# Linear attention before a balanced expert layer: k and v with six rows of every head in 96 partitions

## The chip, the cores and the metric

The kernel runs on one core of a Trainium2 chip. Times are device microseconds of that core; a kernel's time is the median of its runs, and the kernel before has 727.41 us (727.30 to 731.44 in three runs). A core has a matrix engine (TensorE, PE in the profile, with its weight loads as PEld), VectorE (DVE), ScalarE (ACT), GpSimd (POOL) and SyncE (SP), which in this kernel issues the plain transfers. Every engine works through its own list of instructions in order and waits at semaphores for the others. Sixteen DMA engines move the data between HBM and the on-chip SBUF; matmuls write to PSUM.

## The reference

```python
# q, k, v: (8, 8, 576, 64): batch, heads, sequence, head_dim
kv  = np.einsum('bhsd,bhse->bhde', k, v)          # 64 x 64 for each of the 64 heads
out = np.einsum('bhsd,bhde->bhse', q, kv)
rms = np.sqrt(np.mean(out * out, axis=-1, keepdims=True) + 1e-06)
x   = (out / rms * g_norm).transpose(0, 2, 1, 3).reshape(4608, 512)
logits = x @ w_gate                                # 8 experts
# the (token, expert) pairs in falling order of logit; an expert takes 576 tokens at most
assigned = greedy_balanced(logits)
out[assigned == e] = np.maximum(x[assigned == e] @ w1[e], 0) @ w2[e]   # 512 -> 1024 -> 512
```

All is float32.

## The kernel before

It has two stages. The attention stage (up to about 130 us) makes the normalised rows and their gate logits and writes both to `x_dram`; the expert stage finds thresholds for the balanced assignment, gathers each expert's tokens and runs the two layers. The change lies in the attention stage.

`load` brings k, v and q of one batch in two halves each (half of the heads), 576 KB a transfer, in the order k, v, q, k, v, q, all from SyncE. `paced` lets a transfer start only when the one three places before it has landed. A tile has 128 partitions: a pair of heads r, 64 partitions for each head of the pair, and nine sequence rows in every partition. Each of the three names has two buffers, so the loads of batch b+2 are issued at the end of `prepare(b)`, and wait until the matmuls and transposes of batch b have read the buffers.

`prepare(b)` makes what the tiles of batch b need. For each pair of heads it adds up kv in PSUM (L306): the left operand is a 64x64 block of k, the right one of v, and head l of the pair works in its own half of the rows of the matrix engine; even and odd sequence rows j go to the two halves of the columns, so a matmul uses a quarter of the array and the sums of the odd rows end in the upper partitions. ACT copies those down (`odd`, L312), DVE adds (`kv`, L314), and two GpSimd copies (L320) put the sum into both partition halves of `kvx`, the operand of the output matmuls. Four transposes of kv (`t_ps`, L325), an ACT copy (`kvt`, L327) and eight small matmuls with the gate weights (`w_ps`, L333) give kv times gate, which a DVE copy (L335) puts beside kv in `kvx`. `turn_q` transposes q in five pieces (`qt_ps`, L294) that ACT or DVE copies to `qt`. All pieces of PSUM called "tr" share two buffers.

`tiles` makes the output: for each tile of 128 tokens 16 matmuls of 64x64 blocks (`o_ps`, L363), ACT's square and copy (`sq` L369, `o_sb` L370), DVE's sum (`ms` L371), and, once a batch, the norm, the logits and a GpSimd copy of the inverse norm (L388). Head block `9r+j` of `qt` lies in the lower or upper 64 partitions by its parity, which is why kv must stand in both halves.

On PE, DVE, ACT and SP the order is the one in which the program is written: between the tiles of batch b, `prepare(b+1)` advances by one piece at each `yield`, and its rest is done after the last tile. Writes of `o_sb` to `x_dram` are put off: `writes` holds them until there are `2*LAG`, with `LAG + 1` buffers of `o_sb`. The gate weights are loaded on ACT's queue, scaled by g (L116), and a first matmul on PE (`g2_ps`, L198) uses them for a bound on the logits.

Of the kernel before, what the change touches and what calls it, by code (L numbers as in the profile page):

```python
# [7 lines left out]
FT = mybir.dt.float32  # L8
# [3 lines left out]
AL = mybir.AluOpType  # L12
# [3 lines left out]
P = 128  # L16
# [9 lines left out]
def kernel(  # L26
# [11 lines left out]
    nc = tc.nc  # L38
    PS = bass.MemoryType.PSUM

    B, H, S, D = q.shape
    N, DM = out.shape
    E, _, F = moe_w1.shape
    CAP = N // E
    NP = H // 2
    HP = P // 2
    R = S // HP
    GC = N // P
    DC = DM // P
    FC = F // P  # L50
    W = D + E
    NB = (CAP + P - 1) // P
    HALF = CAP // 2
    assert D == HP and R * HP == S and R == 9 and NP == 4 and B % 2 == 0 and GC * P == N and HALF <= 512

    const = ctx.enter_context(tc.tile_pool(name="const", bufs=1, side="left"))
    asg = ctx.enter_context(tc.tile_pool(name="asg", bufs=1, side="left"))
# [4 lines left out]
    att = att_cm.__enter__()  # L64
    psa_cm = tc.tile_pool(name="ps_att", bufs=1, space=PS)
    psa = psa_cm.__enter__()


    loaded = {}
# [3 lines left out]
    def paced(dma):  # L73

        if len(issued) >= AHEAD:
            tc.add_manual_dep(dma.ins, issued[-AHEAD].name,
                              mybir.DependencyInfo(mybir.DependencyClass.Sync, mybir.DependencyReason.DATA),
                              reason="paced loads")
        issued.append(dma.ins)

    def load(name, b, h):

        if h == 0:
            loaded[name, b] = att.tile([P, NP, R, D], FT, name=f"{name}_sb", tag=name, bufs=2)
        rs = slice(h * NP // 2, (h + 1) * NP // 2)
        src = {"k": k, "v": v, "q": q}[name]
        paced(nc.sync.dma_start(
            loaded[name, b][:, rs].rearrange("p r j d -> p r (j d)"),
            src[b].rearrange("h s d -> (h s) d").rearrange("(r p j) d -> p r (j d)", r=NP, j=R)[:, rs]))

    for b in range(2):
        for h in range(2):
# [3 lines left out]
    g_col = const.tile([P, 1], FT, name="g_col")  # L96
    for l in range(2):
        nc.scalar.dma_start(g_col[l * D:(l + 1) * D, :], g_norm.rearrange("(d o) -> d o", o=1))
    gw = const.tile([P, NP, 2, E], FT, name="gw")
    nc.vector.memset(gw, 0.0)  # L100
    for l in range(2):
        ls = slice(l * D, (l + 1) * D)
        nc.scalar.dma_start(gw[ls, :, l, :], moe_w_gate.rearrange("(r p) e -> p r e", p=P)[ls])


    iota_p_i = const.tile([P, 1], I32, name="iota_p_i")
# [7 lines left out]
    ident = const.tile([P, P], FT, name="ident")  # L114
    nc.vector.tensor_scalar(ident, in0=row_f, scalar1=iota_p, scalar2=None, op0=AL.is_equal)
    nc.vector.tensor_scalar(gw.rearrange("p r l e -> p (r l e)"), in0=gw.rearrange("p r l e -> p (r l e)"),  # L116
                            scalar1=g_col, scalar2=None, op0=AL.mult)
    eps = const.tile([P, 1], FT, name="eps")
    nc.vector.memset(eps, EPS)

# [55 lines left out]
    nine, rem, to_row, to_half = (col_at[:, n] for n in range(4))  # L176
    nc.vector.tensor_scalar(nine, in0=row_f[:, 0:GC + 1], scalar1=R - 0.5, scalar2=None, op0=AL.is_gt)
    for i in range(2, B // 2):
# [9 lines left out]
    nc.vector.tensor_tensor(rise, col_at[:, 2:4, 1:GC + 1], col_at[:, 2:4, 0:GC], op=AL.subtract)  # L188


    gsq = asg.tile([P, NP * 2 * E], FT, name="gsq")
    nc.vector.tensor_tensor(gsq, gw.rearrange("p r l e -> p (r l e)"), gw.rearrange("p r l e -> p (r l e)"), op=AL.mult)
    g2 = asg.tile([P, E], FT, name="g2")
    nc.vector.reduce_sum(out=g2, in_=gsq.rearrange("p (a e) -> p e a", e=E), axis=AXX)
    ones_f = asg.tile([P, P], FT, name="ones_f")
    nc.vector.memset(ones_f, 1.0)
    g2_ps = psa.tile([P, E], FT, name="g2_ps", tag="tr", bufs=2)
    nc.tensor.matmul(g2_ps, lhsT=ones_f, rhs=g2, start=True, stop=True)  # L198
    bound = asg.tile([P, 1], FT, name="bound")
    nc.vector.tensor_reduce(bound, g2_ps, axis=AXX, op=AL.max)  # L200
    nc.scalar.activation(bound, bound, ACT.Sqrt)
# [1 line left out]
                            op0=AL.mult, op1=AL.add)  # L203
# [10 lines left out]
    for s in range(NSTEP):  # L214
        nc.vector.tensor_scalar(away[:, s], in0=row_f[:, 0:NCAND + 1], scalar1=span,
                                scalar2=part_of[s], op0=AL.mult, op1=AL.mult)
# [62 lines left out]
    turned_q, kv_of = {}, {}  # L279

    def prepare(b):

        k_sb, v_sb = loaded.pop(("k", b)), loaded.pop(("v", b))

        q_sb = loaded.pop(("q", b)).rearrange("p r j d -> p (r j d)")
        NT = NP * R // 2
        qt = att.tile([P, NT, P], FT, name="qt", tag="qt", bufs=3)
        turned_q[b] = qt

        def turn_q(n):  # L290
            m = min(4, NT - 4 * n)
            t_ps = psa.tile([P, 4, P], FT, name="qt_ps", tag="tr", bufs=2)
            for x in range(m):
                nc.tensor.transpose(t_ps[:, x, :], q_sb[:, (4 * n + x) * P:(4 * n + x + 1) * P], ident)  # L294
            if n in (1, 2):
                nc.vector.tensor_copy(qt[:, 4 * n:4 * n + m], t_ps[:, 0:m])
            else:
                nc.scalar.copy(qt[:, 4 * n:4 * n + m], t_ps[:, 0:m])


        kv_ps = psa.tile([P, 2, 512], FT, name="kv_ps", tag="kv")
        for r in range(NP):
            for j in range(R):
                for l in range(2):
                    ls, cs = slice(l * D, (l + 1) * D), slice(j % 2 * D, (j % 2 + 1) * D)
                    nc.tensor.matmul(kv_ps[cs, l, r * D:(r + 1) * D], lhsT=k_sb[ls, r, j, :], rhs=v_sb[ls, r, j, :],  # L306
                                     start=(j < 2), stop=(j >= R - 2))
            if r < 2:
                turn_q(r)
                yield  # L310
        odd = att.tile([D, 2, NP * D], FT, name="odd", tag="odd")
        nc.scalar.copy(odd, kv_ps[D:P, :, 0:NP * D])  # L312
        kv = att.tile([D, NP, 2, D], FT, name="kv", tag="kv")
        nc.vector.tensor_tensor(kv.rearrange("p r l d -> p l r d"),  # L314
                                kv_ps[0:D, :, 0:NP * D].rearrange("p l (r d) -> p l r d", d=D),
                                odd.rearrange("p l (r d) -> p l r d", d=D), op=AL.add)

        kvx = att.tile([P, H, W], FT, name="kvx", tag="kvx", bufs=3)
        for n in range(2):
            nc.gpsimd.tensor_copy(kvx[n * D:(n + 1) * D, :, 0:D], kv.rearrange("p r l d -> p (r l) d"))  # L320
        yield
        turn_q(2)
        t_ps = psa.tile([P, NP, D], FT, name="t_ps", tag="tr", bufs=2)
        for r in range(NP):
            nc.tensor.transpose(t_ps[:, r, :], kv[:, r].rearrange("p l d -> p (l d)"), ident[0:D, 0:D])  # L325
        kvt = att.tile([P, NP, D], FT, name="kvt", tag="kvt")
        nc.scalar.copy(kvt, t_ps)  # L327
        yield
        turn_q(3)
        w_ps = psa.tile([P, NP, 2 * E], FT, name="w_ps", tag="tr", bufs=2)  # L330
        for r in range(NP):
            for n in range(2):
                nc.tensor.matmul(w_ps[n * D:(n + 1) * D, r], lhsT=kvt[:, r, :],  # L333
                                 rhs=gw[:, r].rearrange("p l e -> p (l e)"), start=True, stop=True)
        nc.vector.tensor_copy(kvx[:, :, D:W], w_ps.rearrange("p r (l e) -> p (r l) e", l=2))  # L335
        kv_of[b] = kvx
        turn_q(4)
        if b + 2 < B:
            for h in range(2):
                for name in "kvq":  # L340
                    load(name, b + 2, h)

    LAG = 5
    writes = []

    def tiles(c0, rows):
# [5 lines left out]
        for t, halves in enumerate(rows):  # L352


            o_ps = psa.tile([P, 2, 512], FT, name="o_ps", tag="o", bufs=2)
            for r2 in range(NP // 2):
                for l in range(2):
                    for rp in range(2):
                        for n, (bn, j) in enumerate(halves):
                            r = 2 * r2 + rp  # L360
                            block = R * r + j
                            ks = slice(block % 2 * D, (block % 2 + 1) * D)
                            nc.tensor.matmul(  # L363
                                o_ps[n * HP:(n + 1) * HP, rp, (2 * r2 + l) * W:(2 * r2 + l + 1) * W],
                                lhsT=turned_q[bn][ks, block // 2, l * HP:(l + 1) * HP],
                                rhs=kv_of[bn][ks, 2 * r + l], start=True, stop=True)
            o4 = o_ps[:, :, 0:NP * W].rearrange("p b (h w) -> p b h w", w=W)
            sq = att.tile([P, H, D], FT, name="sq", tag="sq")
            nc.scalar.activation(sq.rearrange("p (b h) d -> p b h d", b=2), o4[:, :, :, 0:D], ACT.Square, scale=D ** -0.5)  # L369
            nc.scalar.copy(o_sb[:, t].rearrange("p (b h) w -> p b (h w)", b=2), o_ps[:, :, 0:NP * W])  # L370
            nc.vector.reduce_sum(out=ms[:, t * H:(t + 1) * H], in_=sq, axis=AXX)  # L371
            yield
# [40 lines left out]
    with tc.manual_schedule(engines={PE, DVE, ACTE, SPE}):  # L413
        for _ in prepare(0):
            pass
        for b in range(B):
            parts = prepare(b + 1) if b + 1 < B else iter(())
            n = 0
# [368 lines left out]
```

## Time and profile before

| | us |
|---|---|
| median of the runs | 727.41 |
| the profiled execution | 728.39 |
| its span on the core | 726.6 |
| PE busy (share of the span) | 632.7 (87%) |
| DVE busy | 395.3 (54%) |
| ACT busy | 164.4 (23%) |
| POOL busy | 95.8 (13%) |

The profile is of one execution. Its page shows the busy share of each engine in 40 equal slices, the clock that TensorE was granted, and how busy the DMA engines were. The groups of instructions are named by line, engine, operation, output and operands, with the count, the busy time, the mean of one, and the idle time before them with what ended it ("issue" is idle time that no semaphore explains). A matmul of float32 appears as two records here, a transpose as one. In the attention stage (0 to 140 us) the groups are:

| line | what | count | mean ns |
|---|---|---|---|
| L306 | PE `kv_ps`, 64x64 | 1152 | 235 |
| L363 | PE `o_ps`, 64x72 | 1152 | 247 |
| L294 | PE `qt_ps`, 128x128 | 144 | 327 |
| L333 | PE `w_ps`, 128x16 | 128 | 234 |
| L325 | PE `t_ps`, 64x64 | 32 | 257 |
| L312 | ACT `odd`, 64x512 | 8 | 583 |
| L327 | ACT `kvt`, 128x256 | 8 | 375 |
| L314 | DVE `kv`, 64x512 | 8 | 683 |
| L296 | DVE `qt`, 128x512 | 16 | 678 |
| L335 | DVE `kvx`, 128x64 | 8 | 220 |
| L320 | POOL `kvx`, 64x512 | 16 | 608 |
| L388 | POOL `o_sb`, 128x32 | 9 | 240 |

A matmul's duration is that of one from start to end; several run at a time, so the starts of a run of them tell their pace: 36 `kv_ps` records from 22.22 to the next kind of work at 22.90, 32 `o_ps` records from 21.67 to 22.22, four `qt_ps` from 22.90 to 23.49.

### The profile page before, as it was taken

The numbers are of one execution on the slowest core, as the hardware profiler recorded it, in microseconds if no ns is written. First come the engines' busy times: TensorE is split into PE (matmuls) and PEld (weight loads), VectorE is DVE, ScalarE is ACT, GpSimd is POOL, SyncE is SP. The second block draws the span as 40 slices with busy tenths as digits, with TensorE's granted clock in tenths as the row PEclk, the third lists the DMA queues.
The fourth block names the chain that finished last, engine by engine and source line by source line (L and its number), as shares of the span: only waits on it lengthen the run. The fifth ranks groups of instructions, "written<-read, shape, count | busy, mean of one in ns | idle before, by whom it ended". The sixth has DMA issues, their size and how long they took to land.

```text
span 726.6 us, 12295 instructions
## 1 busy us (share of the span) xinstructions
PE 632.7 (87%) x4959; PEld 404.6 (56%) x4959; DVE 395.3 (54%) x1381; ACT 164.4 (23%) x331; POOL 95.8 (13%) x113
## 2 busy tenths in 40 slices
PE   3768686113999999999999999999999999999994
PEld 3656575002774576457546744774576467547641
DVE  4454656886677488748765874787478530010000
ACT  1555565001120211122112112210311122122100
POOL 0100100003002300410041013003100421010011
PEclk9998888555899999999999999999999999999998
DMA  8998888208106300910170045007200945010001
GB/s 290 307 298 287 285 306 312 81 0 259 46 1 229 136 5 1 331 39 1 57 292 23 1 166 197 9 0 275 96 1 3 345 148 179 15 43 8 0 30 36
DMA packets 41400, 93.34 MB, mean 128 GB/s; under 512 B 3456, under 2 KB 3456, under 8 KB 41344
## 3 DMA queue, kind: packets, MB, share of 16 engines
q1 hardware_dynamic: 34752, 72.49, 28.6%
q0 software_dynamic: 5888, 20.06, 7.9%
q8 instruction: 39, 0.64, 0.4%
q14 instruction: 17, 0.14, 0.1%
q10 hardware_dynamic: 704, 0.02, 0.1%
HBM read 72.50 MB, written 20.05 MB: 127 GB/s over the span
## 4 chain that ended last, share of the span: by engine, by line
PE 62%; issue 19%; DVE 11%; POOL 2%; ACT 2%; DMA 2%; ACTq 0%; POOLq 0%; DVEq 0%
PE y_ps L713 23%; PE h_ps L704 23%; PE y_ps L723 3%; PE qt_ps L294 3%; PE o_ps L363 3%; PE kv_ps L306 3%; DVE over L259 2%; PE t_ps L678 2%; PE n_ps L452 2%; POOL out_dram L685 1%; POOL xg L614 1%; DMA gw<-in_moe_w_gate_dram 1%; DVE need L458 1%; DVE ms L371 1%; DVE ends L490 1%
## 5 line engine op out<-in xcount | busy, mean ns | idle before, releaser
L704 PE MATMUL h_ps<-xt,w_sb 128*128 128x288 f32 x1024 | 264.1, 414 | 0.0
L713 PE MATMUL y_ps<-w_sb,hid 128*128 128x512 f32 x512 | 227.6, 595 | 0.0
L704 PEld LDWEIGHTS h_ps<-xt,w_sb 128*128 128x128 f32 x1024 | 191.9, 192 | 54.9 <-issue 5.7
L713 PEld LDWEIGHTS y_ps<-w_sb,hid 128*128 128x128 f32 x512 | 94.2, 190 | 100.8 <-issue 100.0
L707 ACT ACTIVATE hid<-h_ps 128x288 f32<-128x288 f32 x128 | 52.6, 411 | 216.7 <-PE h_ps L704 216.7
L685 POOL DMA_INDIRECT out_dram<-y_sb,outs x40 | 42.9, 1073 | 427.7 <-ACT y_sb L718 399.4
L667 DVE TENSOR_TENSOR xs<-xg 128x512 f32<-128x512 f32 (+1 forms) x40 | 27.4, 689 | 77.7 <-PE t_ps L678 60.0
L259 DVE TENSOR_TENSOR over<-mx,cand 128x1152 bf16<-128x1152 f32 (+3 forms) x52 | 67.0, 1289 | 1.6
L730 DVE TENSOR_TENSOR y_sb<-y_ps,y_part 64x512 f32<-64x512 f32 x8 | 5.5, 682 | 105.2 <-ACT y_part L729 105.2
L718 ACT COPY y_sb<-y_ps 128x512 f32<-128x512 f32 x32 | 18.7, 584 | 161.8 <-PE y_ps L713 161.8
L614 POOL DMA_INDIRECT xg<-x_dram,ids x40 | 39.8, 996 | 77.2 <-DVE at_row L628 35.9
L679 ACT ACTIVATE xt<-t_ps,g_col 128x512 f32<-128x512 f32 (+1 forms) x40 | 25.7, 645 | 95.1 <-PE t_ps L678 87.4
L363 PE MATMUL o_ps<-kvx,qt 64*64 64x72 f32 x1152 | 30.9, 247 | 10.8 <-issue 9.9
L452 PEld LDWEIGHTS <-over 128*128 128x128 bf16 x441 | 17.6, 97 | 40.8 <-DVE over L259 31.7
L452 PE MATMUL n_ps<-best,over 128*128 128x32 bf16 x441 | 19.3, 179 | 23.5 <-DVE over L259 21.0
L678 PEld LDWEIGHTS t_ps<-ident,xs 128*128 128x128 f32 (+1 forms) x160 | 19.6, 150 | 30.6 <-issue 23.1
L371 DVE TENSOR_REDUCE ms<-sq 128x8 f32<-128x512 f32 x36 | 24.0, 679 | 19.7 <-ACT sq L369 19.6
L363 PEld LDWEIGHTS o_ps<-kvx,qt 64*64 64x64 f32 x1152 | 25.0, 149 | 16.6 <-issue 14.8
L294 PE MATMUL qt_ps<-ident,q_sb 128*128 128x128 f32 x144 | 29.1, 327 | 5.3 <-ACT kvt L327 1.9
L306 PE MATMUL kv_ps<-v_sb,k_sb 64*64 64x64 f32 x1152 | 27.1, 235 | 7.5 <-issue 7.5
L490 DVE TENSOR_SCALAR ends<-from_lo,ends 32x2 f32<-32x2 f32 x144 | 31.6, 219 | 2.8
L678 PE MATMUL t_ps<-ident,xs 128*128 128x128 f32 (+1 forms) x160 | 25.0, 283 | 8.6 <-DVE xs L667 8.6
(171 smaller groups left out, 467.2 us busy)
## 6 DMA issues: line engine op xcount, KB each, us to landing
w_sb<-in_moe_w_dram SPq DMA_DIRECT2D x16, 1024.0 KB
w_sb<-in_moe_w_dram SPq DMA_DIRECT2D x8, 2048.0 KB
k_sb<-in_k_dram SPq DMA_DIRECT2D x16, 576.0 KB
v_sb<-in_v_dram SPq DMA_DIRECT2D x16, 576.0 KB
q_sb<-in_q_dram SPq DMA_DIRECT2D x16, 576.0 KB
x_dram<-o_sb SPq DMA_DIRECT2D x16, 576.0 KB
x_dram<-o_sb SPq DMA_DIRECT2D x4, 288.0 KB
xg<-x_dram,ids POOLq DMA_INDIRECT x40
```

The source lines that it names most:

```text
L259: nc.vector.tensor_tensor(over[:, c0:c1], mx[:, c0:c1].rearrange("p (c o) -> p c o", o=1).to_broadcast([P, c1 - c0, NCAND]), cand[:, 1:NCA ...
L294: nc.tensor.transpose(t_ps[:, x, :], q_sb[:, (4 * n + x) * P:(4 * n + x + 1) * P], ident)
L306: nc.tensor.matmul(kv_ps[cs, l, r * D:(r + 1) * D], lhsT=k_sb[ls, r, j, :], rhs=v_sb[ls, r, j, :], start=(j < 2), stop=(j >= R - 2))
L363: nc.tensor.matmul(o_ps[n * HP:(n + 1) * HP, rp, (2 * r2 + l) * W:(2 * r2 + l + 1) * W], lhsT=turned_q[bn][ks, block // 2, l * HP:(l + 1) ...
L452: nc.tensor.matmul(n_ps, lhsT=over[:, c:c + G].rearrange("p c n -> p (c n)"), rhs=best[:, :, c:c + G], start=(c == 0), stop=(c == GC - G))
L490: nc.vector.tensor_scalar(ends[g * QP:(g + 1) * QP], in0=from_lo, scalar1=lo_was[0:QP], scalar2=None, op0=AL.add)
L614: tokens = nc.gpsimd.indirect_dma_start(out=xg[0:nr].rearrange("p h w -> p (h w)"), out_offset=None, in_=x_dram, in_offset=bass.IndirectOf ...
L678: nc.tensor.transpose(t_ps[:, d, 0:nr], xs[0:nr, d * P:(d + 1) * P], ident[0:nr, 0:nr])
L685: put = nc.gpsimd.indirect_dma_start(out=out, out_offset=bass.IndirectOffsetOnAxis(ap=ids_of[t][0:nr, n:n + 1], axis=0), in_=y_sb[0:nr, :] ...
L704: nc.tensor.matmul(h_ps, lhsT=w1[:, 2 * (d % 2) + d // 2, f * P:(f + 1) * P], rhs=xt[:, d, cs], start=(d == 0), stop=(d == DC - 1))
L707: nc.scalar.activation(hid[:, f, cs], h_ps, ACT.Relu)
L713: nc.tensor.matmul(y_ps, lhsT=hid[:, f, a:a + nr], rhs=w2[:, f, :], start=(f == 0), stop=(f == FC - 1))
```

## The change

k and v are loaded with 96 partitions: six sequence rows of every head stand in one partition, for all eight heads. A kv matmul now sums over 96 rows at a time, six for a head instead of nine, and the two heads of a pair go to the two halves of the columns. So kv of head l of every pair ends in partition half l, and one DVE copy takes it to `kvx`; `odd` and `kv` are gone, and the PSUM tile has two buffers. `kvx` is split in two: index 0 holds the heads where they were summed, index 1 the same heads in the other partition half, which two GpSimd copies fill after kv and its gate part are both in place. The transposes turn a pair's 128x64 block at once, the gate matmuls are four instead of eight and work on 64 rows, and their result takes two DVE copies. The gate weights need no zeros and come in one transfer. `LAG` is 4 instead of 5, so the list of writes is shorter by two and `o_sb` has one buffer less. q and the expert stage are as they were.

```diff
     def load(name, b, h):
 
-        if h == 0:
-            loaded[name, b] = att.tile([P, NP, R, D], FT, name=f"{name}_sb", tag=name, bufs=2)
-        rs = slice(h * NP // 2, (h + 1) * NP // 2)
-        src = {"k": k, "v": v, "q": q}[name]
-        paced(nc.sync.dma_start(
-            loaded[name, b][:, rs].rearrange("p r j d -> p r (j d)"),
-            src[b].rearrange("h s d -> (h s) d").rearrange("(r p j) d -> p r (j d)", r=NP, j=R)[:, rs]))
+
+        src = {"k": k, "v": v, "q": q}[name][b]
+        if name == "q":
+            if h == 0:
+                loaded[name, b] = att.tile([P, NP, R, D], FT, name="q_sb", tag="q", bufs=2)
+            rs = slice(h * NP // 2, (h + 1) * NP // 2)
+            paced(nc.sync.dma_start(
+                loaded[name, b][:, rs].rearrange("p r j d -> p r (j d)"),
+                src.rearrange("h s d -> (h s) d").rearrange("(r p j) d -> p r (j d)", r=NP, j=R)[:, rs]))
+        else:
+            if h == 0:
+                loaded[name, b] = att.tile([KP, H, JK, D], FT, name=f"{name}_sb", tag=name, bufs=2)
+            hs = slice(h * H // 2, (h + 1) * H // 2)
+            paced(nc.sync.dma_start(
+                loaded[name, b][:, hs].rearrange("p h j d -> p h (j d)"),
+                src[hs].rearrange("h (p j) d -> p h (j d)", j=JK)))
 
     for b in range(2):
         for h in range(2):
...
     g_col = const.tile([P, 1], FT, name="g_col")
     for l in range(2):
         nc.scalar.dma_start(g_col[l * D:(l + 1) * D, :], g_norm.rearrange("(d o) -> d o", o=1))
-    gw = const.tile([P, NP, 2, E], FT, name="gw")
-    nc.vector.memset(gw, 0.0)
-    for l in range(2):
-        ls = slice(l * D, (l + 1) * D)
-        nc.scalar.dma_start(gw[ls, :, l, :], moe_w_gate.rearrange("(r p) e -> p r e", p=P)[ls])
+    gw = const.tile([D, NP, 2, E], FT, name="gw")
+    nc.scalar.dma_start(gw.rearrange("p r l e -> p (r l) e"), moe_w_gate.rearrange("(h p) e -> p h e", p=D))
 
 
     iota_p_i = const.tile([P, 1], I32, name="iota_p_i")
...
     ident = const.tile([P, P], FT, name="ident")
     nc.vector.tensor_scalar(ident, in0=row_f, scalar1=iota_p, scalar2=None, op0=AL.is_equal)
     nc.vector.tensor_scalar(gw.rearrange("p r l e -> p (r l e)"), in0=gw.rearrange("p r l e -> p (r l e)"),
-                            scalar1=g_col, scalar2=None, op0=AL.mult)
+                            scalar1=g_col[0:D], scalar2=None, op0=AL.mult)
     eps = const.tile([P, 1], FT, name="eps")
     nc.vector.memset(eps, EPS)
 
...
     nc.vector.tensor_tensor(rise, col_at[:, 2:4, 1:GC + 1], col_at[:, 2:4, 0:GC], op=AL.subtract)
 
 
-    gsq = asg.tile([P, NP * 2 * E], FT, name="gsq")
+    gsq = asg.tile([D, NP * 2 * E], FT, name="gsq")
     nc.vector.tensor_tensor(gsq, gw.rearrange("p r l e -> p (r l e)"), gw.rearrange("p r l e -> p (r l e)"), op=AL.mult)
-    g2 = asg.tile([P, E], FT, name="g2")
+    g2 = asg.tile([D, E], FT, name="g2")
     nc.vector.reduce_sum(out=g2, in_=gsq.rearrange("p (a e) -> p e a", e=E), axis=AXX)
     ones_f = asg.tile([P, P], FT, name="ones_f")
     nc.vector.memset(ones_f, 1.0)
     g2_ps = psa.tile([P, E], FT, name="g2_ps", tag="tr", bufs=2)
-    nc.tensor.matmul(g2_ps, lhsT=ones_f, rhs=g2, start=True, stop=True)
+    nc.tensor.matmul(g2_ps, lhsT=ones_f[0:D], rhs=g2, start=True, stop=True)
     bound = asg.tile([P, 1], FT, name="bound")
     nc.vector.tensor_reduce(bound, g2_ps, axis=AXX, op=AL.max)
     nc.scalar.activation(bound, bound, ACT.Sqrt)
...
                 nc.scalar.copy(qt[:, 4 * n:4 * n + m], t_ps[:, 0:m])
 
 
-        kv_ps = psa.tile([P, 2, 512], FT, name="kv_ps", tag="kv")
+        kv_ps = psa.tile([P, NP, D], FT, name="kv_ps", tag="kv", bufs=2)
         for r in range(NP):
-            for j in range(R):
+            for j in range(JK):
                 for l in range(2):
-                    ls, cs = slice(l * D, (l + 1) * D), slice(j % 2 * D, (j % 2 + 1) * D)
-                    nc.tensor.matmul(kv_ps[cs, l, r * D:(r + 1) * D], lhsT=k_sb[ls, r, j, :], rhs=v_sb[ls, r, j, :],
-                                     start=(j < 2), stop=(j >= R - 2))
+                    nc.tensor.matmul(kv_ps[l * D:(l + 1) * D, r], lhsT=k_sb[:, 2 * r + l, j, :], rhs=v_sb[:, 2 * r + l, j, :],
+                                     start=(j == 0), stop=(j == JK - 1))
             if r < 2:
                 turn_q(r)
                 yield
-        odd = att.tile([D, 2, NP * D], FT, name="odd", tag="odd")
-        nc.scalar.copy(odd, kv_ps[D:P, :, 0:NP * D])
-        kv = att.tile([D, NP, 2, D], FT, name="kv", tag="kv")
-        nc.vector.tensor_tensor(kv.rearrange("p r l d -> p l r d"),
-                                kv_ps[0:D, :, 0:NP * D].rearrange("p l (r d) -> p l r d", d=D),
-                                odd.rearrange("p l (r d) -> p l r d", d=D), op=AL.add)
-
-        kvx = att.tile([P, H, W], FT, name="kvx", tag="kvx", bufs=3)
-        for n in range(2):
-            nc.gpsimd.tensor_copy(kvx[n * D:(n + 1) * D, :, 0:D], kv.rearrange("p r l d -> p (r l) d"))
+
+        kvx = att.tile([P, 2, NP, W], FT, name="kvx", tag="kvx", bufs=3)
+        nc.vector.tensor_copy(kvx[:, 0, :, 0:D], kv_ps)
         yield
         turn_q(2)
-        t_ps = psa.tile([P, NP, D], FT, name="t_ps", tag="tr", bufs=2)
+        t_ps = psa.tile([D, NP, P], FT, name="t_ps", tag="tr", bufs=2)
         for r in range(NP):
-            nc.tensor.transpose(t_ps[:, r, :], kv[:, r].rearrange("p l d -> p (l d)"), ident[0:D, 0:D])
-        kvt = att.tile([P, NP, D], FT, name="kvt", tag="kvt")
+            nc.tensor.transpose(t_ps[:, r, :], kvx[:, 0, r, 0:D], ident)
+        kvt = att.tile([D, NP, P], FT, name="kvt", tag="kvt")
         nc.scalar.copy(kvt, t_ps)
         yield
         turn_q(3)
-        w_ps = psa.tile([P, NP, 2 * E], FT, name="w_ps", tag="tr", bufs=2)
+        w_ps = psa.tile([P, NP, 2, E], FT, name="w_ps", tag="tr", bufs=2)
         for r in range(NP):
-            for n in range(2):
-                nc.tensor.matmul(w_ps[n * D:(n + 1) * D, r], lhsT=kvt[:, r, :],
-                                 rhs=gw[:, r].rearrange("p l e -> p (l e)"), start=True, stop=True)
-        nc.vector.tensor_copy(kvx[:, :, D:W], w_ps.rearrange("p r (l e) -> p (r l) e", l=2))
+            nc.tensor.matmul(w_ps[:, r].rearrange("p l e -> p (l e)"), lhsT=kvt[:, r, :],
+                             rhs=gw[:, r].rearrange("p l e -> p (l e)"), start=True, stop=True)
+        for l in range(2):
+            ls = slice(l * D, (l + 1) * D)
+            nc.vector.tensor_copy(kvx[ls, 0, :, D:W], w_ps[ls, :, l])
+        for l in range(2):
+            nc.gpsimd.tensor_copy(kvx[(1 - l) * D:(2 - l) * D, 1], kvx[l * D:(l + 1) * D, 0])
         kv_of[b] = kvx
         turn_q(4)
         if b + 2 < B:
...
                 for name in "kvq":
                     load(name, b + 2, h)
 
-    LAG = 5
+    LAG = 4
     writes = []
 
     def tiles(c0, rows):
...
                             nc.tensor.matmul(
                                 o_ps[n * HP:(n + 1) * HP, rp, (2 * r2 + l) * W:(2 * r2 + l + 1) * W],
                                 lhsT=turned_q[bn][ks, block // 2, l * HP:(l + 1) * HP],
-                                rhs=kv_of[bn][ks, 2 * r + l], start=True, stop=True)
+                                rhs=kv_of[bn][ks, int(block % 2 != l), r], start=True, stop=True)
             o4 = o_ps[:, :, 0:NP * W].rearrange("p b (h w) -> p b h w", w=W)
             sq = att.tile([P, H, D], FT, name="sq", tag="sq")
             nc.scalar.activation(sq.rearrange("p (b h) d -> p b h d", b=2), o4[:, :, :, 0:D], ACT.Square, scale=D ** -0.5)
```

More of the change, by code (lines that the diff above doesn't have):

```diff
@@ L47 @@
     R = S // HP
+    JK = 6
+    KP = S // JK
     GC = N // P
@@ L53 @@
     HALF = CAP // 2
-    assert D == HP and R * HP == S and R == 9 and NP == 4 and B % 2 == 0 and GC * P == N and HALF <= 512
+    assert D == HP and R * HP == S and R == 9 and JK * KP == S and NP == 4 and B % 2 == 0 and GC * P == N and HALF <= 512
     const = ctx.enter_context(tc.tile_pool(name="const", bufs=1, side="left"))
```

## The prediction

> **What bounds the kernel now.** I read the page first. Its 40 slices are 18.2 us each, and the change touches the attention stage, the first seven:
>
> ```profile
> PEclk9998888555899999999999999999999999999998
> DMA  8998888208106300910170045007200945010001
> ...
> q8 instruction: 39, 0.64, 0.4%
> ```
>
> (The last line: queue q8 moved 39 packets, 0.64 MB, 0.4% of the engines' time.) The DMA engines are 80 to 90% busy there, and TensorE's granted clock is below full. Loads could be the bound, so next came the busy time of the engines by stretch, cut where a batch's first `o_ps` starts (columns: stretch, length, PE busy, PEld, DVE, ACT, POOL, clock, DMA share, GB/s):
>
> ```profile
> 92.29:105.53 13.24, 10.56 (x343) 9.01 (x342) 7.23 (x15) 8.26 (x16) 1.46 (x3) 0.91 0.90 328
> 105.53:119.08 13.55, 10.23 (x312) 8.43 (x311) 8.57 (x21) 7.18 (x14) 1.47 (x3) 0.86 0.87 329
> ```
>
> TensorE is the busiest engine, yet idle for 3 us of each batch. Its waits in 10 to 132 us (total, times, longest):
>
> ```profile
> PE o_ps L363 <- issue: 9.9, 4, 4.6
> PE kv_ps L306 <- issue: 7.5, 5, 2.5
> PE t_ps L325 <- DVE kv L314: 2.7, 6, 0.8
> ...
> PE qt_ps L294 <- issue: 1.1, 1, 1.1
> ```
>
> No load is named; 18.5 us are "issue", a wait for nothing the view knows. TensorE's timeline shows where they fall:
>
> ```profile
> 37.57 0.29 PE L306 MATMUL kv_ps<-v_sb,k_sb 64*64 64x64 f32 x4
> 39.51 0.69 PE L306 MATMUL kv_ps<-v_sb,k_sb 64*64 64x64 f32 x32 [1.66 <-issue]
> 40.14 0.66 PE L294 MATMUL qt_ps<-ident,q_sb 128*128 128x128 f32 x4
> 40.72 0.73 PE L363 MATMUL o_ps<-kvx,qt 64*64 64x72 f32 x32
> 41.28 1.10 PE L306 MATMUL kv_ps<-v_sb,k_sb 64*64 64x64 f32 x59
> 43.45 0.39 PE L306 MATMUL kv_ps<-v_sb,k_sb 64*64 64x64 f32 x11 [1.07 <-issue]
> ```
>
> Between the two stalls lie 32+4+32+59 = 127 matmul records, with their weight loads 254 instructions; every other such stall also sits a multiple of 127 records away. The q8 packets are 16 KB[...]. In the trace's DMA records a q8 packet ends at 25.45, 31.13, 38.12 and 42.00 us; TensorE resumes at 26.80, 32.41, 39.51 and 43.45. So **TensorE stalls for its own instructions**. A packet starts 1.1 to 5.8 us (mean 2.9) after TensorE entered the block before, takes about 1.0, and is used about 1.4 later: a cycle of 5.3 us on average. The loads wait for TensorE, not the reverse: SyncE's waits name `qt_ps` for 8.7 us, and batch 7's second k half, issued at 92.81, is used at 109.75.
>
> [...] `kv_ps` records start 15.3 ns apart, `o_ps` 17.2, as their 64 and 72 columns[...]; the switch from `kv_ps` to `qt_ps` costs 0.13 us (18 matmuls take 0.68 instead of 36 x 15.3 ns = 0.55). [...]
>
> **The change, part by part.**
>
> *kv matmuls.* 48 replace 72 a batch, each on half the array instead of a quarter: two side by side, so 2 x 15.3 = 30.6 ns a record. 96 x 30.6 = 2.94 us replaces 144 x 15.3 = 2.20: +0.74 a batch. Bounds: a gain is excluded at full clock, since only three quarters of the rows work; above, if the halves take turns, 5.9 us, +3.7. I take +0.74. Three switches `o_ps` to `kv_ps` and one back are new: 0 to 4 x 0.13, taken 0.25.
>
> *Fold.* `odd` (ACT 583 ns) and `kv` (DVE 683) go; one DVE copy of 128x256 comes, some 0.42 us between 128x64 at 220 and 128x512 at 678. TensorE's wait for `kv` (0.37 a batch, 0.82 in the first) disappears: `qt_ps`, 0.59, hides the copy; without that cover 0.5. -0.37.
>
> *Transposes, gate.* Four transposes stream 128 columns as `qt_ps` does, 4 x 0.147 = 0.59 for 0.39: +0.2. `kvt` grows from 375 to 583 ns, exposed in every second batch: +0.1. `w_ps` halves in number but loads 128 columns: 0.65 us may become 0.3 to 1.0; I take no change.
>
> *GpSimd.* L320's copies ran early; now two follow the last DVE copies, and the second `o_ps` matmul needs them. Behind that wait on TensorE's queue stand the next `kv_ps`, and ACT's `sq`. A 64x288 copy lies between 240 ns (L388, 32 elements) and 608 (512 elements); linear, 436. From the end of `w_ps`: 0.06, copies 2 x 0.18 on DVE of which the second overlaps GpSimd, 0.07, 0.87, 0.06 = 1.25 us to `o_ps`, which starts 0.70 to 0.77 after it now. +0.5 (bounds 0.1 and 0.9).
>
> *gw.* One DMA less on ACT's queue (two take 1.32 us) and no memset. TensorE's first matmul waits for it until 10.77: between 0 and -0.66, taken -0.5, once; the first batch is otherwise neutral, its +1.6 against the shorter fold (0.82, and `odd` off ACT).
>
> *Lag, o_sb with five buffers.* Three writes instead of one go ahead of batch 7's loads on SyncE: 2 x 1.9 = 3.8 us, hidden by the 12 us before their use. ACT's `o_sb` copy of batch 5 waits for batch 0's writes, now issued about 84 us and needed at 93; batch 6's for batch 1's, done some 3 us early. Cost 0; if loads slip that far, ACT and then TensorE wait up to 2 us.
>
> *Loads.* k and v come in 1536-byte packets. The trace's packets of 2048 and 2304 bytes take 84 and 93 ns, on that line 66: 24 x 66 = 1.58 us of each engine for 16 x 93 = 1.49. [...] Bounds: +6% and +40%; a gain has no reason. I take +10%, hidden while a batch lasts over 12.6 us, but it lengthens the fetch's queue by some 0.3 us.
>
> *Instructions.* 326 records a batch become 270: 2.57 blocks become 2.13. From 21.67 to 119.08 seven batches take 13.92 us each. Less 18.5/7 of stalls that is 11.3; the stretches' clocks give 12 us of lost clock, at three quarters busy 1.3 a batch, so 10.0 at full clock. After: 10.0 + 0.74 + 0.25 - 0.37 + 0.3 + 0.5 = 11.4, or 5.4 us a block, where before 3.9 meets a cycle of 5.3. Setting the 17 measured fetch cycles against 5.4 leaves 0.43 of stall a block, 0.6 with the longer queue: 1.3 a batch. With shorter stalls I let lost clock fall to 0.6. Sum 11.4 + 1.3 + 0.6 = 13.3 against 13.92: -0.6 x 7 = -4.3, with gw -4.8. Everything behind attention (batch 7's tiles, the thresholds, the experts) is untouched. The profiled execution took 728.39 us (span 726.6, 1.8 around it): 723.6. The median of the runs, 727.41, lies 1.0 below: 722.6. I say 723.
>
> **The rivals.** *The relief is larger.* The block stays shorter than the fetch because switches are free, `w_ps` is cheaper, the queue no longer: 1.0 to 1.2 us a batch more, 715. For it: half of all blocks wait for fetches today; against it: the batches' longer work.
>
> *The loads take over: slower.* Place: the wait of `kv_ps` for k and v. With k and v at 1.4 times, a batch of loads lasts 11.2 x 3.8/3 = 14.2 us; batch 7's second halves land at 1 + 7.8 x 14.2 + 5.7 for three writes = 118 instead of being used at 109.75: +8, 736. It decides from 1.27 on. For it: DMA at 0.9 busy[...]; against it: 390 GB/s in some stretches, so the engines have room.
>
> *The halves take turns.* +2.9 a batch over my sum, stalls nearly gone: 14.6 x 7 = 102 against 97.4, +3 in the first batch: 736. `w_ps`, already 128x64, shows 29 ns a record for 16 columns, which fits both readings.
>
> *The change does nothing*: excluded, instructions and tiles change.
>
> **How the numbers follow.** Forecast 45% (717 to 729), larger relief 20%, loads 18%, turns 17%. A measurement of this kernel can tell about 1% (7.3 us) from no change. Faster by more: the second case and a tail of the first, 27%; slower by more: most of the last two, 32%; within 1%: 41%. Range: half of the 715 case is left below and a third of the two slow ones above, 714 to 737.
>
> **What would show it.** "issue" waits of `o_ps` and the kv line under 12 us, now 127 records apart again; kv records near 31 ns (61 if they take turns); `o_ps` waiting about half a microsecond for GpSimd at each batch's start; q8 packets 3 or 4 fewer before 130 us; SyncE's waits for k and v near 1.9 us a load[...]. Stalls unchanged at 18 us would make it wrong by +10.

## The result and the profile after

The changed kernel takes 750.04 us (median; 747.15 to 756.06), the kernel before, run beside it, 729.42: a ratio of 1.0292, interval 1.0212 to 1.0373. It is slower by about 20 us. The forecast was 723, its range ended at 737.

The profiled execution has a span of 745.4 us, 18.8 more than before. All of it arises in the attention stage: the last `o_ps` matmul ends at 144.0 us instead of 124.6. The page's lines that answer to those of before:

```profile
PEclk9987877855599999999999999999999999999998
DMA  9999999901600900360073008004500836000001
...
q8 instruction: 35, 0.57, 0.3%
...
PE 52%; DMA 18%; issue 16%; DVE 9%; POOL 2%; ACT 1%; POOLq 0%; SPq 0%; DVEq 0%; ACTq 0%
```

The DMA engines are 90% busy or more in eight slices, where they were at 80% or more in seven, and four instruction packets fewer were moved. The chain that ended last now holds 18% DMA (2% before), and 16% is loads of v. TensorE's waits in 5 to 160 us, in us in total, times, longest:

```profile
PE o_ps L366 <- ACT o_sb L373: 9.4, 5, 4.9
PE kv_ps L313 <- issue: 3.1, 2, 1.9
...
PE kv_ps L313 <- DMA v_sb<-in_v_dram: 1.4, 2, 1.0
PE o_ps L366 <- issue: 1.0, 2, 0.5
PE qt_ps L302 <- DMA q_sb<-in_q_dram: 0.5, 1, 0.5
```

The stalls for instructions are almost gone, 4.1 us where there were 18.5. In their place stands a wait that was 0.8 before: `o_ps` for ACT's copy `o_sb`. The stretches between the first `o_ps` of one batch and the next (length, busy PE, PEld, DVE, ACT, POOL, clock, DMA share, GB/s), for batches 4 to 6 (counted from 0):

```profile
85.28:99.70 14.42, 11.02 (x256) 9.10 (x255) 9.40 (x23) 6.75 (x13) 1.80 (x5) 0.97 1.08 241
99.70:121.89 22.19, 16.68 (x288) 14.13 (x287) 7.31 (x16) 7.71 (x15) 0.51 (x3) 0.64 1.03 259
121.89:138.11 16.22, 12.22 (x255) 10.04 (x254) 8.64 (x22) 6.57 (x13) 1.43 (x5) 0.89 0.97 331
```

The first `o_ps` starts 4.0 us later than before (25.68 for 21.67). Five batches then take 14.80 us each (14.12 before), and the sixth and seventh 22.19 and 16.22 (13.24 and 13.55). So of some 19 us about 7 are spread over the first batches and 12 come in two places near the end. SyncE's timeline (start, duration, idle time left out) tells of the loads and what follows them:

```profile
73.54 0.31 SPq L98 DMA_DIRECT2D k_sb<-in_k_dram  x1
76.09 0.31 SPq L98 DMA_DIRECT2D v_sb<-in_v_dram  x1
78.17 0.39 SPq L91 DMA_DIRECT2D q_sb<-in_q_dram  x1
...
87.68 0.31 SPq L98 DMA_DIRECT2D k_sb<-in_k_dram  x1
...
101.13 0.38 SPq L91 DMA_DIRECT2D q_sb<-in_q_dram  x1
103.93 4.72 SPq L394 DMA_DIRECT2D x_dram<-o_sb  x3
109.75 0.34 SPq L98 DMA_DIRECT2D k_sb<-in_k_dram  x1
```

From the first k load at 0.75 to the seventh batch's at 87.68 a batch of loads takes 14.5 us. Before it took 11.2 early on (first k loads of batches 1 to 3 at 11.05, 22.25 and 33.55), and 11.8 by the same count, which has SyncE's waits for TensorE in it. And the three writes that stand ahead of batch 7's loads start at 103.93, behind the late loads, where the first write of before started at 84.20. ACT's timeline has the two waits that this makes:

```profile
111.19 0.64 ACT L373 COPY o_sb<-o_ps 128x576 f32<-128x576 f32 x1 [8.71 <-DMA x_dram<-o_sb]
...
130.18 0.64 ACT L373 COPY o_sb<-o_ps 128x576 f32<-128x576 f32 x1 [5.80 <-DMA x_dram<-o_sb]
```

Batches 5 and 6 cannot put their first tiles into `o_sb` until batch 0's and batch 1's are written. My theory after this: the 96-partition loads are slow, and the writes are late because of them. Rivals: the shorter lag alone; the kv matmuls themselves, since TensorE's clock is 0.64 to 0.97 here and only 1.9 us of its waits name a load.

### The profile page after: what moved, and what is told of

It is laid out like the page before. It is cut to its first block, busy times and chain, and to the rows that moved or that the text cites. A ratio compares the mean times of both kernels' runs of the same rounds, so it can differ in the third digit from the quotient of the medians.

```text
span 745.4 us, 11400 instructions
## 1 busy us (share of the span) xinstructions
PE 654.2 (88%) x4511; PEld 422.4 (57%) x4511; DVE 395.9 (53%) x1388; ACT 160.8 (22%) x323; POOL 94.6 (13%) x113
## 4 chain that ended last, share of the span: by engine, by line
PE 52%; DMA 18%; issue 16%; DVE 9%; POOL 2%; ACT 1%; POOLq 0%; SPq 0%; DVEq 0%; ACTq 0%
PE y_ps L716 22%; PE h_ps L707 22%; DMA v_sb<-in_v_dram 16%; PE y_ps L726 3%; DVE over L267 2%; PE t_ps L681 2%; PE n_ps L455 2%; POOL out_dram L688 1%; POOL xg L617 1%; DMA x_dram<-o_sb 1%; DVE need L461 1%; DMA w_sb<-in_moe_w_dram 1%; DVE ends L493 1%; ACT y_part L732 0%; DVE y_sb L733 0%
## 5 line engine op out<-in xcount | busy, mean ns | idle before, releaser
L366 PE MATMUL o_ps<-kvx,qt 64*64 64x72 f32 x1152 | 35.1, 262 | 10.9 <-ACT o_sb L373 9.4
L313 PE MATMUL kv_ps<-v_sb,k_sb 96*64 96x64 f32 x768 | 35.9, 262 | 4.6 <-issue 3.1
L366 PEld LDWEIGHTS o_ps<-kvx,qt 64*64 64x64 f32 x1152 | 27.5, 160 | 19.3 <-ACT o_sb L373 10.8
L302 PE MATMUL qt_ps<-ident,q_sb 128*128 128x128 f32 x144 | 30.6, 342 | 6.7 <-DVE kvx L336 3.0
L313 PEld LDWEIGHTS kv_ps<-v_sb,k_sb 96*64 96x64 f32 x768 | 32.1, 172 | 7.7 <-issue 5.7
```

What stands on the lines that cost most here:

```text
L313: nc.tensor.matmul(kv_ps[l * D:(l + 1) * D, r], lhsT=k_sb[:, 2 * r + l, j, :], rhs=v_sb[:, 2 * r + l, j, :], start=(j == 0), stop=(j == JK ...
L366: nc.tensor.matmul(o_ps[n * HP:(n + 1) * HP, rp, (2 * r2 + l) * W:(2 * r2 + l + 1) * W], lhsT=turned_q[bn][ks, block // 2, l * HP:(l + 1) ...
```

## The experiments

A ratio is to the kernel before in the same set of runs; a kernel's own time is its median. "Loads a batch" is the time from the first k load to that of batch 6, over six.

**Everything of the change but the loads.**

```diff
-                loaded[name, b] = att.tile([KP, H, JK, D], ...)
+                loaded[name, b] = att.tile([P, NP * R, D], ...)
...  # loaded as before: 128 partitions, two runs of 576 elements
-  lhsT=k_sb[:, 2 * r + l, j, :], rhs=v_sb[:, 2 * r + l, j, :]
+  at = r // 2 * 18 + (r % 2 * 12 + 2 * j + l) % 18
+  lhsT=k_sb[0:KP, at, :], rhs=v_sb[0:KP, at, :]
```

> The changed kernel with the loads of before: k and v again come as 128 partitions with 2304-byte packets, and every kv matmul takes 96 rows of some 64-wide block of them, so that instructions, tiles and waits are those of the changed kernel while the values of kv are not the reference's. Theory 'loads' (the 96-partition loads, 14.5 us a batch instead of 11.2, cost the time and the late writes follow from them): 720 to 728 us, loads near 11.5 us a batch, ACT's wait for x_dram under 1 us. Rival 'lag' (three writes ahead of the last loads are enough): 738 to 745, with a wait of ACT for x_dram of over 5 us. Rival 'matmul' (K of 96 rows on two column halves, at half clock most of the time): 740 to 750, kv records and granted clock as in the changed kernel.

Measured: 728.31 us, ratio 0.9932 (0.9911 to 0.9952), loads 11.9 us a batch, no wait of ACT for `x_dram`, although the lag is 4. TensorE's waits in 5 to 140 us:

```profile
PE kv_ps L314 <- DMA q_sb<-in_q_dram: 1.5, 1, 1.5
PE kv_ps L314 <- issue: 1.5, 1, 1.5
...
PE o_ps L367 <- ACT o_sb L374: 1.1, 2, 0.8
PE o_ps L367 <- issue: 0.5, 1, 0.5
```

With k and v loaded in 128 partitions, 2.9% slower turns into 0.7% faster. The loads are the cause, and the matmuls are not. TensorE's wait view alone would have acquitted the loads, for it names them for 1.9 us only. From the first `o_ps` of batch 0 to that of batch 7 the changed kernel takes 112.4 us, this one 91.1, so 21.3 us are lost. TensorE's waits for `o_sb`, for loads and for "issue" grow from 4.6 us here to 15.4 there, about half of that. The rest goes with a slower TensorE: its granted clock in 25 to 123 us is 0.92 here and 0.81 there. Why the clock is lower with slow loads is not shown.

**The lag, in both kernels.** In the changed one `LAG` is 5 again (`kvt` and `part` give a buffer each for the room); in the kernel before it is 4.

```diff
-    LAG = 4
+    LAG = 5
```

> The changed kernel with LAG 5, so that one write stands ahead of batch 7's loads and o_sb has six buffers again; room comes from one buffer of kvt and of part instead of two. Theory 'loads': ACT's 14.5 us of waiting for x_dram go, and the loads of 14.5 us a batch remain: 739 to 744. Rival 'lag': back to 724 to 731. Rival 'matmul': 745 to 750.

> The kernel before with LAG 4 alone. Theory 'loads': the writes are early enough when loads take 11.2 us a batch, within 1% of before. Rival 'lag': slower by 5 to 10 us, with a wait of ACT for x_dram.

Measured: 744.99 us, ratio 1.0168 (1.0114 to 1.0221), against 1.0292 (1.0212 to 1.0373) for the changed kernel. The medians are 5 us apart, but the intervals overlap and the last `o_ps` ends at 143.1 us for 144.0, so what the lag is worth when loads are late is not clear of noise. In the kernel before it is worth nothing that can be told: 0.9987 (0.9952 to 1.0021). ACT's wait, which I expected to go with lag 5, stays where loads are slow:

```profile
ACT o_sb L373 <- DMA x_dram<-o_sb: 9.9, 1, 9.9
```

**What makes the loads slow.** First, packets against partitions: 128 partitions with packets of 1536 bytes, and 96 with 3072.

```diff
# a_128x1536, on a_load128
-  src....rearrange("(r p j) d -> p r (j d)", r=NP, j=R)
+  rows.rearrange("(c p j) d -> p c (j d)", p=P, j=6)
# a_96x3072, on the changed kernel
-  src[hs].rearrange("h (p j) d -> p h (j d)", j=JK)
+  rows.rearrange("(c p j) d -> p c (j d)", p=KP, j=2 * JK)
```

> k and v in 128 partitions, but in 1536-byte packets as in the changed kernel (three for each partition and load, 384 in all); kv matmuls as in a_load128, so the values of kv are not the reference's. Theory 'partitions' [...]: 722 to 730 us, loads 11.2 to 12 us a batch. Rival 'packets' (384 packets of 1536 bytes are slower than 256 of 2304): 742 to 752, loads 14 us a batch.

> k and v in 96 partitions in packets of 3072 bytes, 192 for a load; everything else is that of the changed kernel, the rows in a partition are others, so the values of kv are not the reference's. Theory 'partitions': 744 to 752 us, loads 14 us a batch. Rival 'packets': 720 to 728, loads about 11 us a batch.

Measured: 727.78 us, 0.9940 (0.9916 to 0.9964), loads 11.8 us a batch; and 746.93 us, 1.0235 (1.0167 to 1.0302), loads 14.3. It is the partitions; in 128 of them packets of 1536 bytes cost nothing that can be told.

Then their place: the second pair of heads of every load is put into partitions 32 to 127, against a control with the same pieces in 0 to 95.

```diff
-    AHEAD = 3
+    AHEAD = 6
...
+            for r in range(h * NP // 2, (h + 1) * NP // 2):
+                at = r % 2 * SHIFT          # 32, or 0 in the control
+                paced(nc.sync.dma_start(
+                    loaded[name, b][at:at + KP, 2 * r:2 * r + 2].rearrange("p h j d -> p h (j d)"),
+                    src[2 * r:2 * r + 2].rearrange("h (p j) d -> p h (j d)", j=JK)))
```

> The changed kernel with every load cut in two (a pair of heads each, six pieces in flight instead of three whole loads); the second pair of each load goes to partitions 32 to 127 instead of 0 to 95[...]. The kv matmuls of those pairs take only the 64 rows from partition 64 on, a third of their sum is left out. Theory 'ports' [...]: loads 11.2 to 12.3 us a batch, 720 to 731 us. Rival[...] (any transfer of 96 partitions is slow, wherever they lie): loads 14 to 15 us a batch, 742 to 753.

> The same pieces and the same number in flight, but every pair stays in partitions 0 to 95; the kv matmuls of the second pairs take the 64 rows from partition 0 on, so a third of their sum is left out here too. Both theories: loads 14 to 15 us a batch, 742 to 753 us. [...]

Measured: 746.55 us, 1.0209 (1.0143 to 1.0275), and 745.37 us, 1.0223 (1.0139 to 1.0306); loads 14.3 us a batch in both. Moving half of the pieces to partitions 32 to 127 changes nothing, and that speaks against my estimate for the loads, which I had made from the share that partitions 0 to 63 take, two thirds here. Whether the two pieces are under way at the same moment isn't seen here. The next runs test that share in another way.

Last, other numbers of partitions, each with 2304-byte packets.

```diff
+    LP = 112                                # and 120
-  loaded[name, b][:, rs]...
+  loaded[name, b][0:LP, rs]...              # rows: LP * 18 of the 2304 of a half
```

> a_load128 with k and v in 112 partitions, 2304-byte packets as there, seven eighths of the bytes of k and v; the values of kv are not the reference's. In 15 to 60 us a_load128 moves 305 GB/s with 2304-byte packets of 111 ns on average, the changed kernel 234. Theory 'shares' [...] slow too, 230 to 260 GB/s and packets over 130 ns. Rival 'fewer ports' (a transfer is slowed in the measure in which it leaves partitions out): 285 to 305 GB/s, packets of 100 to 118 ns.

> The same with 120 partitions, fifteen sixteenths of the bytes. [...] theory 'shares' [...]: 270 to 300 GB/s, packets of k and v near 111 ns. Rival 'fewer ports': 295 to 305 GB/s. If it is as slow as 112 or slower, the number of partitions to an engine is not what matters, but that it is not 128.

Both ran once, 729.3 and 752.65 us beside 732.81, and their loads are smaller by an eighth and a sixteenth, so the rates count, and each is of one execution. The stretch 15 to 60 us, first with 128 partitions, then 112, then 120, then the changed kernel with 96 (the last two columns are DMA share and GB/s):

```profile
15.00:60.00 45.00, 42.47 (x872) 35.83 (x869) 22.07 (x61) 20.48 (x40) 3.04 (x8) 0.89 0.93 307
```

```profile
15.00:60.00 45.00, 42.61 (x858) 35.43 (x855) 21.55 (x54) 21.14 (x41) 3.03 (x8) 0.89 1.00 265
```

```profile
15.00:60.00 45.00, 40.97 (x758) 33.96 (x756) 21.00 (x66) 19.40 (x37) 3.02 (x8) 0.85 0.99 233
```

```profile
15.00:60.00 45.00, 41.40 (x765) 33.85 (x763) 21.06 (x64) 19.60 (x37) 3.04 (x8) 0.89 1.02 236
```

The expectations count packets of loads alone, 305 and 234 GB/s for the 307 and 236 of the view. In the DMA records a 2304-byte packet of that stretch takes 111 ns on average with 128 partitions, 138 with 112, 155 with 120 (most packets with 128 take 93). With 96 a 1536-byte packet takes 113 ns, against 74 in `a_128x1536`. So neither theory holds as stated: 'shares' had 230 to 260 GB/s for 112 and 270 to 300 for 120, its rival 285 to 305 and 295 to 305, and 120 leaves the fewest partitions out and is the slowest. My estimate from the share of partitions 0 to 63 falls as well: of 96, 112 and 120 partitions, 67, 57 and 53% are partitions 0 to 63, and the rates, 236, 265 and 233 GB/s, don't follow that order. What is shown is that each of 96, 112 and 120 partitions makes the packets longer, those of q beside them too (137 ns in the changed kernel), and that 128, the only other number tried, does not. Why is open: no run here sees which engines carry a transfer.

**The instruction fetch.** The prediction's other pillar was that TensorE waits for its instructions behind the loads in flight. Fewer and more of them:

```diff
-    AHEAD = 3
+    AHEAD = 2    # b_ahead2, kernel before;   a_ahead5: 5, changed kernel
```

> The kernel before with two loads in flight instead of three. Theory 'fetch queue' (TensorE's instruction blocks wait behind the loads in flight): the waits put down to 'issue' in 10 to 132 us fall from 18.5 to about 10 us, 717 to 724. Rival: the fetch delay doesn't depend on the loads in flight, and the loads get slower with fewer of them: 728 to 735.

> The changed kernel with five loads in flight instead of three. Theory 'partitions' as a limit of throughput: little changes, 744 to 752 us, loads over 13.5 us a batch. Rival 'latency' (with three in flight the engines that finish a load early have nothing to do, deeper queues fill that): loads 11.5 to 12.5 us a batch, 728 to 738, with more waits put down to 'issue' on TensorE.

Measured: 740.26 us, 1.0097 (1.0067 to 1.0128), and 753.64 us, 1.0306 (1.0246 to 1.0366), both above every range named for them. TensorE's waits in 5 to 140 us with two in flight in the kernel before:

```profile
PE qt_ps L294 <- DMA q_sb<-in_q_dram: 10.7, 7, 3.5
PE kv_ps L306 <- DMA v_sb<-in_v_dram: 10.1, 7, 2.5
...
PE o_ps L363 <- ACT o_sb L370: 8.2, 4, 6.1
...
PE o_ps L363 <- issue: 1.4, 2, 1.1
```

and in 5 to 145 us with five in the changed one:

```profile
PE kv_ps L313 <- issue: 6.7, 2, 3.7
PE o_ps L366 <- issue: 6.3, 2, 3.3
PE w_ps L332 <- issue: 3.8, 1, 3.8
```

The stalls go with the loads in flight: 18.5 us become 1.4 with two, and 4.1 become 16.8 with five. Two things are mixed in this. With two, TensorE waits 20.8 us for loads, and part of its fetches may be hidden in those waits; how much is not shown. But the fetch starts earlier as well: from the first matmul of a block (each 127th record) to the start of the next q8 packet it takes 1.61 us on average with two loads in flight, 2.45 with three (18 and 19 blocks before 128 us). The total went the other way than I expected: with two, the loads take 14.5 us a batch and become the bound. ACT then waits for `x_dram` in the kernel before too, though its lag is 5:

```profile
ACT o_sb L370 <- DMA x_dram<-o_sb: 13.1, 1, 13.1
```

With five in the changed kernel ACT has no such wait, and SyncE's waits name TensorE:

```profile
SPq L91 <- PE qt_ps L302: 25.6, 6, 8.2
SPq L98 <- PE kv_ps L313: 22.1, 5, 10.2
```

So its loads, 15.2 us a batch, wait for TensorE there; their rate in 15 to 60 us rises from 236 to 249 GB/s only. Halving the loads gives steps in between:

```diff
+        for r in range(h * NP // 2, (h + 1) * NP // 2):   # k, v and q: one pair of heads, 288 KB
+            paced(nc.sync.dma_start(loaded[name, b][:, r]...
-    AHEAD = 3
+    AHEAD = 5    # b_quart5;   6 in b_quart6
```

> The kernel before with each load cut into two of 288 KB and five of them in flight, 1.4 MB instead of 1.7. Theory 'fetch queue': the fetch delay follows the bytes in flight, 'issue' waits fall from 18.5 to 5 to 12 us, loads stay under 12.5 us a batch and 719 to 726. Rival: what the fetch gains the loads lose, as with two in flight: 730 to 738.

> The kernel before with each load cut into two of 288 KB and six in flight, as many bytes as before. Theory 'bytes in flight' (b_quart5 gained because 1.4 MB instead of 1.7 stand ahead of the instruction fetch): within 0.4% of before, 729 to 735 us. Rival 'pieces' (the smaller loads themselves gain, kv starts after the first pair): as b_quart5, 0.5 to 1% faster than before.

Measured: 726.68 us, 0.9925 (0.9892 to 0.9957), and 730.23 us, 0.9997 (0.9964 to 1.0030). With fewer bytes in flight the kernel gains 0.8%, with the smaller pieces alone nothing; the two intervals lie just apart. The first is faster than both kernels and computes the same. That its gain comes from shorter fetches isn't shown: its profiled execution, the slowest of its ten at 729.6 us, has 15.4 us of "issue" waits where I expected 5 to 12, and one wait of 7.0 for v; the second has 15.7.

## Why the prediction was wrong

Its own steps, one by one:

*What bounds the kernel now* was right, and so was the direction in which the change moves it. Records between stalls, packets on q8 (35 for 39) and the fall of "issue" waits came as said. With the loads of before, seven batches take (115.53 - 24.41)/7 = 13.02 us, for which the sum had 13.3, and the kernel gains 0.7% of 729, 5.0 us, for which it had 4.8. That the totals lie so near is in part luck. The "issue" waits left there are 2.0 us, 0.3 a batch, where the sum had 1.3; so the rest of a batch took 12.7 us for 12.0. And the first batch cost what the sum did not have (below).

*The prices on the engines* held, as the groups of the changed kernel in 0 to 160 us show (columns as in the page):

```profile
L332 PE MATMUL w_ps<-gw,kvt 64*128 64x16 f32 x64 | 8.5, 262 | 0.0
...
L338 POOL COPY kvx<-kvx 64x288 f32<-64x288 f32 x16 | 6.8, 424 | 116.3 <-DVE kvx L336 115.8
...
L320 DVE COPY kvx<-kv_ps 128x256 f32<-128x256 f32 x8 | 3.4, 423 | 7.9 <-PE kv_ps L313 7.9
```

The GpSimd copy takes 424 ns (436), the DVE copy 423 (420). At TensorE's full pace 48 kv records start within 1.40 us, 29.7 ns apart (30.6): the halves run side by side, and that rival falls. `w_ps` takes 1.06 us, past the upper end of 0.3 to 1.0. The +0.5 for GpSimd does not show: `o_ps` waits 0.2 us in all for its copies in a_load128 and never in the changed kernel. One term was missed: the first batch, called neutral, costs 2.7 us in a_load128 (24.41 for 21.67), though only 0.6 in a_128x1536 (22.28). The 0.5 us for gw is gained in neither: TensorE's first matmul starts at 11.30 and 10.82 (10.77). Part of the 2.7 shows in the kv records: in the first batch of a_load128 and of the changed kernel they start 53.5 ns apart, half pace, while before they were 29.2 ns apart for the first 72 and 16.4 for the other 72. So kv alone takes 96 x 53.5 = 5.14 us there for 72 x 29.2 + 72 x 16.4 = 3.28: +1.9 us, where the sum had +0.74 a batch. It isn't that the halves take turns, for four `qt_ps` take 1.12 us in that stretch and 0.66 later. Why TensorE keeps that pace longer there is open; the view gives its clock as 1.00.

*Loads: "I take +10%, hidden while a batch lasts over 12.6 us"* is the step that failed. A batch of loads takes 14.5 for 11.2, +29%. Put on k and v alone, as the rival "the loads take over" counts, that is 1.44 times: past its break-even of 1.27 and above the upper bound of +40%. (Counted so, +10% makes 11.9 us; where the 12.6 comes from is not worked out.) The sum gave an engine 24 x 66 ns for its packets of a load; a packet takes 113. The +10% was my estimate, made from the share of the bytes that goes to partitions 0 to 63, by which the loads fitted within the pace of before. No run shows that this share sets the time: a_shift takes 14.3 us a batch like its control, and 112 and 120 partitions, at 265 and 233 GB/s, don't follow it.

*Lag: "Cost 0; if loads slip that far, ACT and then TensorE wait up to 2 us"* failed with it. ACT waits 14.5 us, and the two batches concerned last 9.0 and 2.7 us longer than before. The wait comes with slow loads, at either lag: 9.9 us with lag 5 (a_lag5), and 13.1 in the kernel before with two loads in flight; with fast loads there is none at lag 4 (a_load128, b_lag4), and at 265 GB/s in between it is 6.7 (a_load112). The sum had named the users of the writes, the `o_sb` of batches 5 and 6, and a slack of 3 to 9 us; the loads ahead of the first write came 20 us later than before (103.93 for 84.20), and that took all of it.

The rival "the loads take over" had the sign but not the place: `kv_ps` waits for v for 1.4 us in all. Its landing of batch 7's second halves at 118 us is near (v is issued at 118.46 and lands after that). It put 736 because it knew of no wait behind the writes and of no lower clock.

## What to carry to other kernels

A transfer's shape is a price to measure, not to derive: leaving 8, 16 or 32 partitions of 128 out cost 14 to 24% of the DMA rate here (233, 265 and 236 GB/s for 307), at every packet size tried. Where writes stand behind loads on one queue, price both at the pessimistic end of the loads, for late loads use up the slack of the writes (the first write started at 103.93 us here for 84.20). And TensorE's "issue" waits at a fixed count of instructions (127 matmul records) were its own instruction fetch here: with two loads in flight instead of three they shrank from 18.5 to 1.4 us, and the loads themselves were late, 14.5 us a batch for 11.8.

## What the runs showed of the hardware

- With k and v in 96, 112 or 120 partitions the core's transfers ran at 236, 265 and 233 GB/s in 15 to 60 us, with all in 128 at 307; 128 partitions gave 308 with 1536-byte packets, and 96 gave 250 with 3072-byte ones. A packet of 1536 bytes took 113 ns with 96 partitions and 74 with 128; the records here don't name the engines.
- TensorE can be busy 13.99 of 14.10 us in a batch (71.18 to 85.28 in the changed kernel) and yet be slow: its clock was 0.76 there.
- Instruction stalls of 18.5, 1.4, 4.1 and 16.8 us went with 3 and 2 loads in flight in the kernel before, 3 and 5 in the changed one.
- TensorE's granted clock in 25 to 123 us was 0.81 with slow loads and 0.92 with fast ones, with the same instructions (changed kernel, a_load128).
